# One weight load cut so that 2.5 of 8 heads come in short loads on fewer DMA engines

## Chip, cores, metric

One core of a Trainium2 chip. The metric is the device time of one execution in microseconds; the kernel before takes 206.0 us (median of 6 runs, 205.80 to 206.13). The profiled execution has a span of 204.1 us.

## The reference, cut to what matters

One decoding step of a transformer block for one token: attention of 32 heads over a cache of 4096 keys and values, the projection `wo`, a residual, then a GeGLU layer.

```python
q = (layernorm(x) @ wq)                       # 640 -> 32 heads x 128
o = softmax(q k^T * 128 ** -0.5) v            # k_cache, v_cache: 32 x 4096 x 128, bf16
h = x + o.reshape(1, 1, 32 * 128) @ wo        # wo: 4096 x 640
out = h + (gelu(ln(h) @ w_gate) * (ln(h) @ w_up)) @ w_down
```

The bytes decide it: 84.2 MB are read from HBM (the chip's large memory), 67 MB of them keys and values, and each is used once.

## The kernel before

All loads go out on one queue, that of SyncE, in the order in which they are used. `wo` comes in four groups of 8 heads, 128 partitions (rows of SBUF, the on-chip memory that the loads write) of 10240 B each. Only the group's load and the wait for it matter here.

```python
P, D, HG = 128, 640, 8
wo_t = sb("wo", [P, HG, D], bf16)

def load(name, dst, src):
    SP.dma_start(dst, src).then_inc(S[name], 16)
...
def load_wo(g):
    SP.wait_ge(S["pe"], pe_at(2 * g, "project"))
    src = A_wo[g * HG * P : (g + 1) * HG * P, :].rearrange("(p j) d -> p j d", p=P)
    load("wo", wo_t[:], src)

load("wq", wq_sb, ...)
load("x", x4[0:P:32, :], ...)                  # 4 rows
load_k(0)
for m in range(NQ):                            # 8 quads of heads
    load_k(m + 1)                              # 128 x 32768 B (cut: the last ones come in halves)
    load_v(m)
    if m % 2 == 1:
        load_wo(m // 2)
load("wg", ...); load("wu", ...)               # then w_down in six loads of 64 rows, odd and even partitions
...
if m % 2 == 1:                                 # on VectorE, before the projection
    DVE.wait_ge(S["wo"], 16)
    DVE.sem_inc(S["wo"], -16)
```

The softmax here doesn't subtract the row's maximum and nothing guards it: scores larger than these inputs give would overflow.

Of the kernel before, what the change touches and what calls it, by code (L numbers as in the profile page):

```python
# [9 lines left out]
def kernel(  # L10
# [19 lines left out]
    PE, DVE, ACT, SP, POOL = nc.tensor, nc.vector, nc.scalar, nc.sync, nc.gpsimd  # L30

    P = 128
    D = 640
# [5 lines left out]
    NQ = NH // QH  # L39
# [8 lines left out]
    PAIRS = NQ // 2  # L48
    HG = 2 * QH
    DF = 1728  # L50
    PER = 2
    PAIR_UNITS = PER * DF // P
    NFC = (PAIR_UNITS + 1) // 2
    HALVES = D // PER
    COLS = NFC * HP
    WD = ((0, 8), (8, 11), (11, 14))
    RG = DF // YR
    EPS = 1e-5
    SCALE = DH ** -0.5
    GELU_C = 0.044715  # L60
# [5 lines left out]
    def sb(name, shape, dtype=f32):  # L66
        return pool.tile(shape, dtype, name=name, tag=name)

    wo_t = sb("wo", [P, HG, D], bf16)
    TILE = NB * DH  # L70
    W_MLP = DC * DF
    big = sb("big", [P, (SLOTS + 2) * TILE + 2 * W_MLP], bf16)
# [14 lines left out]
    ones_f = sb("ones_f", [P, P])  # L87
    parity = sb("parity", [P, PER])
    mean_f = sb("mean_f", [P, P])
# [31 lines left out]
    e2 = sb("e2", [P, NFC])  # L121
    g_own = sb("g_own", [P, PER])
    hid = sb("hid", [P, NFC], bf16)
    hid_own = sb("hid_own", [P, PER], bf16)
    g_col = sb("g_col", [P, NFC, HP])
# [27 lines left out]
    S = {n: nc.alloc_semaphore(f"s_{n}") for n in names}  # L153
# [7 lines left out]
    def spare(engine):  # L161

        i = next(spares)
        return engine.memset(spare_t[:, i : i + 1], 0.0)  # L164

    def wait(engine, which, value):
        if value > 0:
            engine.wait_ge(S[which], value)
# [13 lines left out]
    def wait_pe(value):  # L182
        DVE.wait_ge(S["pe"], value)

    def dve(make, raw=True):

        if raw:
            wait(DVE, "dve", done["dve"])
        return tick("dve", make())
# [11 lines left out]
    with nc.allow_low_precision(reason="sums of one 1 and zeros"):  # L201
        dve(lambda: DVE.reduce_sum(row_of[:], by_c, AX.X), False)
        dve(lambda: DVE.reduce_sum(col_of[:], by_c.rearrange("p c j -> p j c"), AX.X), False)
        dve(lambda: DVE.reduce_sum(parity[:], ident[:].rearrange("p (i b) -> p b i", b=PER), AX.X), False)
        dve(lambda: DVE.reduce_sum(of_head[:], by_w, AX.X), False)
# [9 lines left out]
    def var_of(m, v):  # L215

        dve(lambda: DVE.tensor_tensor(v[:], m[:, 0:1], m[:, 0:1], op=ALU.mult))
        dve(lambda: DVE.tensor_tensor(v[:], m[:, 1:2], v[:], op=ALU.subtract))
        return dve(lambda: DVE.tensor_single_scalar(v[:], v[:], EPS, op=ALU.add))  # L219

# [134 lines left out]
    def pe_at(m, name):  # L355

        return T["quad", name] + m * per_turn
# [31 lines left out]
    def up(ps, w, name):  # L389
# [3 lines left out]
        for j in range(DC):  # L393
            for r in range(YR):
                rhs = w[:, j, r * RG : (r + 1) * RG].rearrange("p (i f) -> p i f", f=PAIR_UNITS)
                rhs = bass.AP(
# [54 lines left out]
    def load(name, dst, src):  # L451
        SP.dma_start(dst, src).then_inc(S[name], 16)  # L452
# [28 lines left out]

    def load_wo(g):
        SP.wait_ge(S["pe"], pe_at(2 * g, "project"))
        src = A_wo[g * HG * P : (g + 1) * HG * P, :].rearrange("(p j) d -> p j d", p=P)
        load("wo", wo_t[:], src)

    load("wq", wq_sb, A_wq.rearrange("(p c) n -> p c n", c=DC))
    SP.wait_ge(S["dve"], DVE_X4)
# [2 lines left out]
    for m in range(NQ):  # L491
        if m + 1 < NQ - 1:
            load_k(m + 1)
        else:
            load_last_k(m + 2 - NQ)
# [3 lines that stand above are left out]
# [4 lines left out]
    for i, (a, b) in enumerate(WD):  # L503
        for odd in range(PER):
            start, end_at = max(a * D, odd * HALVES), min(b * D, (NFC - 1) * D + HALVES + odd * HALVES)
            at = (PAIR_UNITS // 2) * D * odd
# [16 lines left out]
    def spread():  # L523
        shape = [P, HG, P // HG]
        return DVE.tensor_tensor(
            o_spread[:],
            o_col[:].unsqueeze(2).broadcast_to(shape),
            row_of[:].unsqueeze(1).broadcast_to(shape),
            op=ALU.mult,
        )  # L530
# [10 lines left out]
    def own_queries(m):  # L541
        shape = [P, 2, 2, QH]
        dve(
            lambda: DVE.tensor_tensor(
                q_to,
                q_at[:, m].unsqueeze(3).broadcast_to(shape),
                of_head[:].unsqueeze(1).unsqueeze(1).broadcast_to(shape),
                op=ALU.mult,
            ),
            False,  # L550
        )

    def turn_keys(m, half):
        to = kt.bitcast(f32).rearrange("p (k c j n) -> p c j k n", k=2, c=NC, n=HP)
        of = kr[m % SLOTS].bitcast(f32).rearrange("p (c x) -> p c x", c=NC)
        if half == 0 or m == NQ - 1:
            name = f"k{m % SLOTS}{'b' if half else ''}"
            DVE.wait_ge(S[name], 16)
            DVE.sem_inc(S[name], -16)
        for c in range(half * HALF, (half + 1) * HALF):  # L560
            DVE.transpose(to[:, c], of[:, c].rearrange("p (j k n) -> p j k n", k=2, n=HP)).then_inc(S["kt"], 1)  # L561
# [5 lines left out]
    for m in range(NQ):  # L567
        own = slice(QH * (m % 2), QH * (m % 2 + 1))
        wait_pe(pe_at(m, "s"))
        assert dve(lambda: DVE.transpose(s_turned[:].rearrange("p j n -> p (j n)"), s_bank[:]), False) == D_SCORES[m]  # L570
        wait_pe(pe_at(m, "e"))
        shape = [P, NB, QH]
        DVE.tensor_tensor(  # L573
            e_t[:],
            e_ps.unsqueeze(2).broadcast_to(shape),
            of_head[:].unsqueeze(1).broadcast_to(shape),
            op=ALU.mult,
        ).then_inc(S["dve_pe"], 1)
        dve(lambda: DVE.reduce_sum(rs_row[:], e_ps, AX.X), False)
        wait(DVE, "dve", done["dve"])  # L580
        DVE.tensor_scalar(rs_cur[:], of_head[:], rs_row[:], None, op0=ALU.mult).then_inc(S["dve_pe"], 1)  # L581
        if m + 1 < NQ:
            own_queries(m + 1)
            turn_keys(m + 1, 0)
        wait_pe(pe_at(m, "totals"))
        dve(lambda: DVE.reciprocal(rinv[:], t_ps), False)
        wait_pe(pe_at(m, ("pv", 1)))
        dve(lambda: DVE.tensor_tensor(o_col[:, own], o_ps, rinv[:], op=ALU.mult))  # L588
        wait(DVE, "dve", done["dve"])
        (spread() if m % 2 == 1 else spare(DVE)).then_inc(S["dve_pe"], 1)  # L590
        wait_pe(pe_at(m, "reorder"))
        if m % 2 == 1:
            DVE.wait_ge(S["wo"], 16)
            DVE.sem_inc(S["wo"], -16)
        (DVE.tensor_copy(o_row[:], r_ps) if m % 2 == 1 else DVE.memset(o_row[:], 0.0)).then_inc(S["dve_pe"], 1)  # L595
        if m + 1 < NQ:
            turn_keys(m + 1, 1)
# [81 lines left out]
```

## Time and profile before

| | before |
|---|---|
| median of 6 runs | 206.00 us |
| span of the profile | 204.1 us |
| read from HBM | 84.23 MB, 413 GB/s over the span |
| last w_down load landed | 200.68 us |
| busiest compute engine | DVE, 52% of the span |

The page's slices of the kernel before: each digit is the busy share of one fortieth of the span in tenths, for the DMA engines the mean of 16; the second line is what they moved.

```profile
DMA  7999999999998999999989999999999999999980
GB/s 249 393 475 417 411 430 469 437 411 416 437 446 381 473 450 411 424 424 456 443 370 478 437 411 430 437 443 437 395 427 424 430 433 421 433 425 429 419 369 20
```

From the second slice on, the DMA engines are busy for 80% or more of every slice but the last. The end of the chain of waits (start us, us, what) of the kernel before says the same:

```profile
175.22 0.60 SPq L452
175.82 0.04 issue
175.86 24.81 DMA big<-in_B_w_down_dram
200.68 0.04 issue
200.72 0.41 PE y L378 x12
201.13 0.02 issue
201.15 0.33 DVE y_row L630
```

The last load was issued 24.8 us before it landed: it stood in a queue. What follows it takes less than a microsecond and the store. So the kernel's time is the time at which the last of 16 DMA engines is done.

The trace also holds every DMA packet (start, duration, size, but not the engine) and every landing. Two things can be worked out from them. First, a 32768 B packet takes 1214 ns at the median (10th to 90th percentile 1213 to 1221), and most packets start 3 to 4 ns before another ends, so packets can be chained into 16 engines. Second, the 16 engines are not level. How much later than the first engine each one landed, for three loads of the kernel before (us, my tally):

```
V load, first engine at  44.3 us: 15 within 0.49, then 1.03
K load, first engine at 170.3 us: 12 within 0.46, then 0.94  1.00  1.63  2.04
w_up,   first engine at 193.4 us: 12 within 0.48, then 1.06  1.65  1.96  2.07
```

Four engines are late, and everything waits for the last. One of them started late; the other three had stood still for an instruction fetch, whose packets are on queues of their own (q8 with 16 KB, q14 with 8 KB, lines of the DMA part of the page):

```profile
q1 hardware_dynamic: 4240, 84.23, 96.7%
q8 instruction: 3, 0.05, 0.1%
q14 instruction: 2, 0.02, 0.0%
```

The columns are packets, MB and share. The share looks like nothing, but a fetch of 16 KB took about 1.09 us, one of 8 KB 0.32 us, and the load packet behind it on the same engine is stretched too (1681 ns after a 16 KB one, 1873 after the 8 KB one at 49.9 us, instead of 1213).

The load of `wo`'s first group has its issue and the next one here (SyncE's timeline of the kernel before, 53 to 60 us):

```profile
53.98 0.33 SPq L452 DMA_DIRECT2D wo<-in_A_wo_dram  x1
59.10 0.33 SPq L452 DMA_DIRECT2D big<-in_A_k_cache_dram  x1
```

### The profile page before, as it was taken

The page shows a single profiled execution, that of the slowest core. Times are in us where ns is not written, and L with a number is a line of the kernel's source. Part 1 is how long each engine was busy: PE and PEld are TensorE (multiplying, and loading weights), DVE is VectorE, ACT ScalarE, POOL GpSimd, SP SyncE. Part 2 cuts the span into 40 slices and gives each one's busy share as a digit, 9 for nine tenths or more (in the row PEclk, how much of TensorE's full clock was granted, in tenths as well). Part 3 has the DMA queues.
Part 4 walks back from the last instruction along what each step waited for, and adds up shares of the span by engine and source line. Part 5 has one row for each costly group of instructions (what it writes and reads, how often), then busy time and mean ns, then how long its engine had stood idle before and what let it go on. Part 6 is the DMA issues. An engine that isn't in the chain of part 4 may idle for free. (4 is left out here: it accounts for less than half of the span.)

```text
span 204.1 us, 4083 instructions
## 1 busy us (share of the span) xinstructions
PE 87.7 (43%) x1837; PEld 53.6 (26%) x1839; DVE 105.2 (52%) x185; ACT 4.6 (2%) x11; POOL 6.8 (3%) x12
## 2 busy tenths in 40 slices
PE   0003404406621861066407640482166468257972
PEld 0001101105311711063107310451063164046220
DVE  5003498570658278309480957065908492732360
ACT  2000100000000000000000000000000000000000
POOL 8301000000000000000000000000000000000100
PEclk9999955555585585555555555558555555555698
DMA  7999999999998999999989999999999999999980
GB/s 249 393 475 417 411 430 469 437 411 416 437 446 381 473 450 411 424 424 456 443 370 478 437 411 430 437 443 437 395 427 424 430 433 421 433 425 429 419 369 20
DMA packets 4245, 84.30 MB, mean 413 GB/s; under 512 B 528, under 2 KB 528, under 8 KB 784
## 3 DMA queue, kind: packets, MB, share of 16 engines
q1 hardware_dynamic: 4240, 84.23, 96.7%
q8 instruction: 3, 0.05, 0.1%
q14 instruction: 2, 0.02, 0.0%
HBM read 84.23 MB, written 0.00 MB: 413 GB/s over the span
## 5 line engine op out<-in xcount | busy, mean ns | idle before, releaser
L561 DVE STREAM_TRANSPOSE big<-big 128x1024 f32<-128x1024 f32 x64 | 73.8, 1211 | 6.3 <-issue 3.8
L273 PE MATMUL o<-ex,big 128*128 128x4 bf16 x1024 | 28.6, 166 | 38.7 <-PEq L173 38.7
L273 PEld LDWEIGHTS o<-ex,big 128*128 128x128 bf16 x1024 | 28.4, 104 | 39.1 <-issue 39.1
L245 PE MATMUL s<-big,q_quad 128*8 128x512 bf16 x256 | 27.9, 579 | 24.0 <-DVE big L561 24.0
L588 DVE TENSOR_TENSOR o_col<-o,rinv 128x4 bf16<-128x4 f32 x8 | 1.3, 163 | 38.9 <-PE o L273 38.9
L245 PEld LDWEIGHTS s<-big,q_quad 128*8 128x8 bf16 x256 | 7.0, 111 | 40.1 <-DVE big L561 31.9
L570 DVE STREAM_TRANSPOSE s_turned<-s 128x512 f32<-128x512 f32 x8 | 5.7, 717 | 13.5 <-PE s L245 13.5
L280 PE MATMUL a<-wo,o_row 128*1 128x160 bf16 x256 | 9.9, 333 | 2.3 <-DVE o_row L595 2.3
L573 DVE TENSOR_TENSOR ex<-e,of_head 128x512 bf16<-128x512 f32 x8 | 5.5, 692 | 6.8 <-PE e L261 6.8
L292 PE MATMUL t<-rs_cur,ones_f 128*128 128x4 f32 x16 | 4.7, 365 | 10.1 <-DVE rs_cur L581 10.1
L280 PEld LDWEIGHTS a<-wo,o_row 128*1 128x1 bf16 x256 | 7.2, 115 | 3.0 <-DVE o_row L595 3.0
L302 PE MATMUL o<-x_col,mean_f 128*128 128x10 f32 x2 | 0.6, 376 | 16.8 <-DVE x_col L210 16.8
L292 PEld LDWEIGHTS t<-rs_cur,ones_f 128*128 128x128 f32 x16 | 4.0, 312 | 11.0 <-DVE rs_cur L581 11.0
L261 PE MATMUL e<-e_part,ident 128*32 128x32 bf16 x128 | 2.5, 197 | 10.0 <-PEq L340 10.0
L445 POOL TENSOR_TENSOR hr<-hv,half_f 128x1 f32<-128x1 f32 x1 | 0.6, 554 | 172.2 <-DVE hv L219 172.2
L223 DVE CAST x_row<-x_69 128x160 f32<-128x160 bf16 x1 | 0.2, 244 | 11.6 <-DMA x_69<-in_A_x_dram 11.6
L261 PEld LDWEIGHTS e<-e_part,ident 128*32 128x32 bf16 x128 | 1.8, 106 | 16.0 <-issue 16.0
L513 ACT ACTIVATE e_part<-s_turned 128x128 bf16<-128x128 f32 x8 | 2.5, 309 | 154.1 <-DVE s_turned L570 154.1
L302 PEld LDWEIGHTS o<-x_col,mean_f 128*128 128x128 f32 x2 | 0.5, 313 | 16.8 <-DVE x_col L210 16.8
L295 PE MATMUL o<-col_of,o_spread 128*128 128x8 bf16 x8 | 1.5, 188 | 6.8 <-issue 3.3
L441 POOL MEMSET wo<- 128x5120 bf16 x1 | 4.4, 4370 | 0.0
L318 PE MATMUL g<-big,xn_bf 128*1 128x512 bf16 x20 | 2.8, 546 | 1.9 <-DVE xn_bf L230 1.9
(84 smaller groups left out, 45.7 us busy)
## 6 DMA issues: line engine op xcount, KB each, us to landing
big<-in_A_k_cache_dram SPq DMA_DIRECT2D x7, 4096.0 KB, 20.6
big<-in_A_v_cache_dram SPq DMA_DIRECT2D x6, 4096.0 KB, 17.7
big<-in_A_v_cache_dram SPq DMA_DIRECT2D x4, 2048.0 KB, 11.9
big<-in_A_wq_dram SPq DMA_DIRECT2D x1, 5120.0 KB, 15.2
wo<-in_A_wo_dram SPq DMA_DIRECT2D x4, 1280.0 KB, 15.8
big<-in_A_k_cache_dram SPq DMA_DIRECT2D x2, 2048.0 KB, 17.6
big<-in_B_w_gate_dram SPq DMA_DIRECT2D x1, 2160.0 KB, 18.5
big<-in_B_w_up_dram SPq DMA_DIRECT2D x1, 2160.0 KB, 23.2
```

The costliest lines, as they stand in the source:

```text
L245: inst = PE.matmul(s_bank[32 * r : 32 * r + 2 * QH, :], lhsT=q_quad[:, 2 * k + e, (1 - b) * QH : (3 - b) * QH], rhs=kt_at[:, k, HALF * b + ...
L261: inst = PE.matmul(to[32 * h : 32 * h + 32, r], lhsT=ident[:, 32 * r : 32 * r + 32], rhs=e_part[:, :, :, h], start=True, stop=True, tile_p ...
L273: inst = PE.matmul(o_ps, lhsT=vt[:, j, :], rhs=e_t[:, j, :], start=(j == 0), stop=(j == NB - 1))
L280: inst = PE.matmul(attn_ps[32 * r : 32 * r + 1, :], lhsT=o_row[:, j : j + 1], rhs=wo_t[:, j, r * YW : (r + 1) * YW], start=False, stop=j = ...
L292: mark("totals", PE.matmul(ps, lhsT=ones_f[:], rhs=rs_cur[:], start=True, stop=True))
L295: inst = PE.matmul(ps, lhsT=o_spread[:].rearrange("p h c -> p (h c)"), rhs=col_of[:], start=True, stop=True)
L318: inst = PE.matmul(qr_ps[b][32 * r : 32 * r + 1, :], lhsT=xn_bf[:, c : c + 1], rhs=wq_sb[:, c, :].rearrange("p (m h d) -> p m h d", h=QH, ...
L441: POOL.memset(t[:], 0.0).then_inc(S["pool"], 1)
L513: ACT.activation(e_part[:].rearrange("p b j h -> p j b h"), s_turned[:, :, 0 : 2 * QH].rearrange("p j (b h) -> p j b h", b=2), AF.Exp, sca ...
L561: DVE.transpose(to[:, c], of[:, c].rearrange("p (j k n) -> p j k n", k=2, n=HP)).then_inc(S["kt"], 1)
L570: assert dve(lambda: DVE.transpose(s_turned[:].rearrange("p j n -> p (j n)"), s_bank[:]), False) == D_SCORES[m]
L573: DVE.tensor_tensor(e_t[:], e_ps.unsqueeze(2).broadcast_to(shape), of_head[:].unsqueeze(1).broadcast_to(shape), op=ALU.mult,).then_inc(S[" ...
```

## The change

The intent, as far as the diff shows it: level the 16 engines. 40 rows can't be shared evenly by 16 engines. In the changed kernel's trace a load of 40 rows landed 10 times, one of 8 rows 8 times, one of 128 rows 16 times, so that many engines carried them. And never more than ten of the group's 3200 B packets are in flight at once there, though three loads of 40 rows stood in line: so I take it that all three ran on the same ten. The other six then have less to do. The trace gives the engines no numbers. Those here are names: 0 to 3 for the four that carry the 4 rows of x, 0 to 7 for those of the loads of 8 rows, 0 to 9 for those of 40, 10 to 15 for the rest. That each of these sets lies within the next, and is the same for every load of its size, is an assumption.

```diff
+    WO_PART = 5 * D // 2
+    WO_LOADS = [[(slice(0, P), slice(0, HG * D))] for _ in range(NQ // 2)]
+    WO_LOADS[0] = [(rows, slice(0, WO_PART)) for rows in (*[slice(i, 120, 3) for i in range(3)], slice(120, P))]
+    WO_LOADS[0] += [(slice(0, P), slice(WO_PART, HG * D))]
...
-        src = A_wo[g * HG * P : (g + 1) * HG * P, :].rearrange("(p j) d -> p j d", p=P)
-        load("wo", wo_t[:], src)
+        src = A_wo[g * HG * P : (g + 1) * HG * P, :].rearrange("(p j) d -> p (j d)", p=P)
+        dst = wo_t[:].rearrange("p j d -> p (j d)")
+        for rows, at in WO_LOADS[g]:
+            load("wo", dst[rows, at], src[rows, at])
...
-            DVE.wait_ge(S["wo"], 16)
-            DVE.sem_inc(S["wo"], -16)
+            DVE.wait_ge(S["wo"], 16 * len(WO_LOADS[m // 2]))
+            DVE.sem_inc(S["wo"], -16 * len(WO_LOADS[m // 2]))
```

## The prediction

> What bounds the kernel now: the DMA stream. In the page's slices the 16 DMA engines are about 99% busy from start to end (413 GB/s over the span), no compute engine is over 52%, and the chain of waits ends in 24.8 us of the last w_down load, landed at 200.68 us; only 0.41 us of matmul, 0.33 us of DVE and the store follow. The queue never runs dry: K and V loads land 12 to 21 us after issue.
>
> The engines run independently at one rate. In the trace's DMA packet records a 32768 B packet takes 1213 ns (10th to 90th percentile 1213 to 1221), and the last packets, when most engines have finished, are no faster. So the slowest engine sets the end, not the sum of bytes. Of each load's 16 landings 12 come within 0.48 us, four at 0.94, 1.01, 1.61 and 2.02 us. I chained packets end to start to see why: one late engine started late, the others stood still for an instruction fetch (16 KB at 50.0 and at 56.5 us, about 1.1 us each; 8 KB at 49.9 and 190.7 us). At the end these four are 1.05, 1.61, 1.92 and 2.02 us behind the first.
>
> What the change does. [...] So 128 rows use 16 engines, 40 rows 10, 8 rows 8. This trace agrees in one place: the 4-row load of x has four updates beside the sequencer's own, and four engines carry its 320 B packets. In the first 2.5 heads of group 0 (3200 B a row), engines 0-7 take 13 rows instead of 8, engines 8-9 take 12, engines 10-15 none. Bytes and matmuls stay.
>
> Cost by engine. Now: 8 packets of 10240 B at 385 ns, 3.08 us. After: 8 of 7040 B, about 267 ns (estimate between 3200 B at 126 ns and 10240 B), 2.13 us, plus 13 or 12 of 126 ns. Engines 10-15: -0.95 us; 0-7: +0.69; 8-9: +0.57. Four more issues of about 0.5 us on SP at 54 us: its next load waits until 59.1 us, so free. DVE's wait for wo lies 1.5 us after its landing: free. Only each engine's position at the end counts.
>
> So it depends on where the late four sit. The prompt twelve may take 0.69 us: they end at most 1.2 us behind the first. If all four are among 10-15, the end comes 0.95 us earlier (about 205.1 us); that is surely the intent. But the engine 1.61 us late carried a packet of x[...]. It would be 2.30 us behind, against 2.02 now: +0.3 us (206.4), even if the other three are relieved. If one of the two latest is below 10 too, +0.65 us (206.7). Chaining could have swapped two engines, and fetches could fall elsewhere, so I give the improvement 40%.
>
> Prediction: 206.2 us, 8 in 10 between 205.1 and 206.9; faster by over 2%: 1%, within 2%: 98%, slower: 1%.
>
> Signs. 192 packets of 3200 B instead of 64, 10240 B ones fewer by 128. In loads after wo group 0 the spread of landings changes: a late engine among 10-15 gains 0.95 us, one below 10 loses 0.6 to 0.7. The last w_down landing moves as the last engine's lag does.
>
> Wrong if the short loads use other engines, small packets collide on SBUF and cost over 126 ns, fetches fall on other engines, or the queue runs dry.

The sum came to 206.2 us. For an engine of 0 to 7 it is 13 packets of 126 ns less 0.95 us, +0.69 us; for the late one among them 1.61 + 0.69 - 2.02, the +0.3 us (206.4) that is weighed against a gain of 0.95 us (205.1). That loads of 40 and 8 rows use 10 and 8 engines is shown by the landings of the changed kernel (10, 10, 10 and 8).

## More of the kernel before

The columns that matter are the last two, the share of busy DMA engines and GB/s (counted by the packets that start in a stretch, so short stretches scatter by some per cent and a share may pass 1):

```profile
core 0: us, PE busy (x) PEld busy (x) DVE busy (x) ACT busy (x) POOL busy (x), PEclk, DMA share, GB/s
59.00:63.00 4.00, 0.90 (x18) 0.72 (x18) 3.11 (x7) 0.31 (x1) 0.00 (x0) 0.57 0.95 410
63.00:67.00 4.00, 1.12 (x43) 1.15 (x43) 2.76 (x4) 0.00 (x0) 0.00 (x0) 0.50 1.04 438
```

## The result

The changed kernel takes 208.26 us (median of 6 runs, 207.98 to 208.45) against 206.00 us: 2.26 us more, ratio 1.0109 (95% interval 1.0096 to 1.0122). That is within 2%, but far outside the range of the prediction. A ratio here is the mean time of one kernel's fast runs over that of the other's fast runs of the same rounds, so it is not quite the ratio of the medians.

The end of the chain of waits of the changed kernel:

```profile
177.12 0.04 issue
177.16 25.77 DMA big<-in_B_w_down_dram
202.93 0.04 issue
202.97 0.41 PE y L382 x12
203.38 0.02 issue
203.41 0.33 DVE y_row L636
```

The matmul and the addition behind the load take the same 0.41 and 0.33 us. The landing has moved from 200.68 to 202.93 us, and that is the whole difference. The loads' issue is not it. SyncE's timeline of the changed kernel, 53 to 60 us:

```profile
54.00 3.22 SPq L456 DMA_DIRECT2D wo<-in_A_wo_dram  x5
59.12 0.33 SPq L456 DMA_DIRECT2D big<-in_A_k_cache_dram  x1
```

Five issues take 3.2 us, but the next load goes out at 59.12 instead of 59.10 us, as predicted. The slices of the changed kernel:

```profile
DMA  7999999999999999999999999999999999999970
GB/s 246 437 429 406 457 451 413 406 476 430 403 413 308 467 419 413 432 464 419 413 403 460 432 445 438 413 432 445 390 436 429 419 441 422 429 425 429 423 316 10
```

The busy digits are all nines, as before. In the line below, the thirteenth slice (61.9 to 67.1 us, where the group's packets are) has 308 instead of 381 GB/s. The two stretches of the changed kernel show it better:

```profile
59.00:63.00 4.00, 0.90 (x18) 0.73 (x18) 3.11 (x7) 0.31 (x1) 0.00 (x0) 0.54 0.94 401
63.00:67.00 4.00, 0.00 (x0) 0.01 (x1) 2.77 (x4) 0.00 (x0) 0.00 (x0) 0.50 1.01 269
```

From 63 to 67 us all 16 engines are busy (share 1.01) and move 269 GB/s instead of 438. They work at packets that do not get on. In the packet records the 3200 B packets took a median 204 ns (126 at best), the 7040 B ones 335 (267 at best, 556 at worst), and four 32768 B packets of late engines, in flight at the time, took 1721 to 2062 instead of 1213 ns. Summed over 62.5 to 76.5 us against a stream of 430 GB/s, 1.54 us of the stream are lost; in the kernel before 0.00.

The landings that answer to those shown before (us behind the first engine, my tally):

```
K load, first engine at 170.9 us: 0.02 0.05, then 11 from 1.32 to 1.82, then 2.13  2.72
w_up,   first engine at 194.0 us: 0.03 0.06, then 11 from 1.31 to 1.87, then 2.20  3.75
```

Three engines run ahead: the prompt ones among the relieved. The other 13 are behind, and the last gets another microsecond between the two loads, from the 8 KB fetch at 191.8 us.

Two theories were open after this. A: engines collide where they write, so that a packet's time depends on the partitions that it and the packets beside it write. B: small pieces, or rows of HBM read in two pieces, are slow in themselves. And two sizes: how much of the 2.26 us is collisions, and how much the uneven share of a late engine among 0 to 9.

The expectations put theory A in terms of lanes: the partitions that, as I assumed, one and the same engine writes in a load of 128 rows. Which engine writes which partitions no run shows. The runs show which destinations are slow and which are not.

### The profile page after: what moved, and what is told of

Read it like the earlier page. It is cut to its first block, busy times and chain, and to the rows that moved or that the text cites. A ratio compares the mean times of both kernels' runs of the same rounds, so it can differ in the third digit from the quotient of the medians.

```text
span 206.4 us, 4089 instructions
## 1 busy us (share of the span) xinstructions
PE 89.1 (43%) x1839; PEld 53.5 (26%) x1839; DVE 105.2 (51%) x185; ACT 4.5 (2%) x11; POOL 6.8 (3%) x12
## 5 line engine op out<-in xcount | busy, mean ns | idle before, releaser
L405 PE MATMUL g<-big,hc 128*1 128x448 bf16 x20 | 3.9, 1001 | 0.1
```

Source lines behind the costliest of these rows:

```text
L405: inst = PE.matmul(ps[32 * r : 32 * r + 1, :].rearrange("q (c i b) -> q i b c", c=NFC, b=PER), lhsT=hc[:, j : j + 1], rhs=rhs, start=False ...
```

## The experiments

All kernels were correct by the comparison with the reference. For e2, e3 and e5, which leave data out on purpose, this only says that the comparison's tolerance covers the missing or misplaced part, not that the result is right. Times are medians; "lost" is lost stream time in 62.5 to 76.5 us, as above; packet times are medians.

| run | time, us | before, same rounds | ratio, 95% | 3200 B packet, ns | lost, us |
|---|---|---|---|---|---|
| changed kernel | 208.26 | 206.00 | 1.0096 to 1.0122 | 204 | 1.54 |
| e1 two pieces | 206.11 | 206.02 | 0.9988 to 1.0021 | 126 | 0.03 |
| e2 own lanes | 206.18 | 206.02 | 0.9992 to 1.0025 | 126 | 0.02 |
| e3 other lanes | 207.75 | 206.02 | 1.0071 to 1.0105 | 234 | 1.21 |
| e5 uneven, own lanes | 206.59 | 205.99 | 1.0019 to 1.0046 | 126 | 0.02 |
| e6 more on 0-3 | 206.55 | 205.99 | 1.0017 to 1.0045 | none | 0.00 |
| e7 five heads | 210.11 | 205.99 | 1.0182 to 1.0214 | 414 (6400 B) | 3.02 |
| e8 blocks of 40 | 208.38 | 205.99 | 1.0100 to 1.0131 | 155 | 1.45 |
| e9 32 rows, every fourth | 206.13 | 206.02 | 0.9997 to 1.0028 | 126 | 0.04 |
| e10 one head | 207.15 | 206.02 | 1.0045 to 1.0072 | 66 (1280 B) | 0.62 |
| e11 blocks of 32 | 208.03 | 205.94 | 1.0081 to 1.0115 | 221 | 2.10 |
| e12 every eighth | 208.06 | 205.94 | 1.0090 to 1.0134 | 205 | 2.08 |

### e1: two pieces of 128 rows

```diff
-    WO_LOADS[0] = [(rows, slice(0, WO_PART)) for rows in (*[slice(i, 120, 3) for i in range(3)], slice(120, P))]
+    WO_LOADS[0] = [(slice(0, P), slice(0, WO_PART))]
```

> Group 0 of wo as two loads of 128 rows each (3200 B and 7040 B of a row), so the pieces are cut as in the changed kernel but every engine takes 8 rows of both. Theory A (short loads make engines write partitions of other engines' SBUF lanes and they collide): no dip, 3200 B packets 126 ns, 7040 B 267 ns, time 206.1 us (before 206.0). Theory B (small pieces, or reading a row of HBM in two pieces, are slow in themselves): 3200 B packets about 200 ns and 7040 B over 400 ns as in the changed kernel, time 207.5 us or more.

206.11 us, packets of 126 and 267 ns. Small pieces cost nothing. Theory B falls.

### e2 and e3: the same loads, 64 partitions apart

```diff
+    SHIFT = 0        # e3: 64
-    WO_LOADS[0] = [(rows, slice(0, WO_PART)) for rows in (*[slice(i, 120, 3) for i in range(3)], slice(120, P))]
+    WO_LOADS[0] = [(slice(h + i, h + 32, 4), slice(0, WO_PART)) for h in (0, 32) for i in range(4)]
...
-            load("wo", dst[rows, at], src[rows, at])
+            to = slice(rows.start + SHIFT, rows.stop + SHIFT, rows.step) if rows.step else rows
+            load("wo", dst[to, at], src[rows, at])
```

> Wrong result on purpose (partitions 64 to 127 of the first 1600 columns are not loaded). Eight loads of 8 rows, each on engines 0-7[...]. Theory A: 3200 B packets stay near 126 ns and the stream stays at 425 to 432 GB/s. Theory B and a theory C (order of HBM rows): 3200 B packets slow, near 200 ns, dip of the stream to about 250 GB/s. Time by A between 205.1 and 206.2 us, as the late engines fall.

> Wrong result on purpose. Same loads, same source rows, same engines 0-7 as in e2_own_lanes; only the destination is 64 partitions higher[...]. Theory A: packets of 3200 B about 200 ns or more, 7040 B ones over 400 ns, the stream dips to about 250 to 300 GB/s, and it ends 0.8 us or more after e2_own_lanes. Theories B and C: the same as e2_own_lanes within 0.2 us, with the same packet times.

Stretches of e2:

```profile
59.00:63.00 4.00, 0.90 (x18) 0.72 (x18) 3.17 (x6) 0.28 (x1) 0.00 (x0) 0.50 0.97 418
63.00:67.00 4.00, 1.34 (x51) 1.38 (x52) 2.62 (x4) 0.00 (x0) 0.00 (x0) 0.50 1.03 430
```

Stretches of e3:

```profile
59.00:63.00 4.00, 0.90 (x18) 0.73 (x18) 3.11 (x7) 0.31 (x1) 0.00 (x0) 0.55 0.94 401
63.00:67.00 4.00, 0.14 (x5) 0.17 (x6) 2.87 (x4) 0.00 (x0) 0.00 (x0) 0.50 1.02 297
```

Same source rows, same sizes, same order, same number of engines; only the partitions written differ by 64. The stream from 63 to 67 us is 430 against 297 GB/s, a 3200 B packet 126 against 234 ns, and the time 206.18 against 207.75 us. The cause is on the side of the destination, and it depends on which partitions are written; an order of rows in HBM (theory C of the expectation) falls with it. This is the experiment that settles the kind of the loss. e2 also shows a second thing: its engines 8 to 15 have 0.95 us less to do (they miss the eight packets and have 7040 B ones for the rest), yet the end does not come earlier. So one of the latest engines is among 0 to 7.

A rival remains: that writing these partitions is slow for the engines of the short loads by themselves, without another engine in their way. The packets of e3 speak against it. The first short packet starts at 63.1 us, so no engine with eight of them can be through (8 times 126 ns) before 64.1 us. If all eight short loads run on the same eight engines, the twelve 7040 B packets that start before then must be those of the other eight, whose destination is the same as in e2, and nine of them took 400 to 529 ns instead of 267. The engines that carry none of the short loads lose too.

### e4: which engines are late

```diff
+    mark_t = sb("mark", [16, 1920], bf16)
...
         if m % 2 == 1:
             load_wo(m // 2)
+        if m == 1:
+            for k in range(1, 16):
+                load("mark", mark_t[0:k, 8 * k * (k - 1) : 8 * k * (k + 1)], A_wq[0:k, 0 : 16 * k])
```

(On the kernel before. Simplified here: the run has a semaphore of its own for these loads, and a wait for it at the end.)

> The kernel before with 15 tiny loads of 1 to 15 rows behind wo group 0 (32 B a row for each row of the load, so the size tells the load): an engine's packets tell its number. One look at which engines are the late four. My prediction's reading: one of them is among 0-3, the other three are among 10-15. Rival: the fetches fall on other engines from one execution to the next, and the changed kernel's profile already has them swapped (there the 8 KB fetches seem to hit an engine of x). Time 206 to 206.6 us.

This failed. 208.46 us in one run of unknown state: after fifteen loads of a few kB the engines were idle for part of the time (share 0.88 from 66 to 70 us, 339 GB/s). SyncE's timeline of e4:

```profile
52.83 0.33 SPq L453 DMA_DIRECT2D wo<-in_A_wo_dram  x1
53.20 5.26 SPq L453 DMA_DIRECT2D mark<-in_A_wq_dram  x15
58.51 0.40 SPq L453 DMA_DIRECT2D big<-in_A_k_cache_dram  x1
```

The K load behind them was issued at 58.5 us, yet between 66.6 and 68.5 us mostly 7 to 12 of 16 engines had a packet, and the small ones came some 0.3 us apart, load after load. The markers are too disturbed to give numbers to engines. It is a different loss from that of the change, in whose trace 16 engines are busy all the time (share 1.01 from 63 to 67 us).

The question was settled another way. In the packet records, a fetch starts 3 to 4 ns before the packet ends behind which its engine then stands still. With that rule each fetch falls on one chain. I chained all 14 profiles this way. In 12 of them, those of both kernels included, the 8 KB fetch at about 49 to 50 us stopped an engine that carries a packet of x, so one of 0 to 3; in e8 the chain broke there, and in e1 it came out as an engine without x, which I can't explain. (A second chaining, with the semaphore packets taken in and a start 2 to 5 ns before an end, gave 13 of 14, e1 and e8 included, with e4 the exception. A single chain can swap engines, so the position rests on e6 below.) The two 16 KB fetches before 60 us stopped engines without x in all 14. My first chaining, in the prediction, had swapped the two fetches that start 112 ns apart. So the engine among 0 to 3 is not the one that is 1.61 us late, but the one that the 8 KB fetches hit twice: 0.95 us late until 190.7 us, 1.92 us at the end.

### e5: the uneven share alone

```diff
 (as e2, and)
+    extra_t = sb("extra", [P, 8000], bf16)
+        if g == 0:
+            load("wo", extra_t[0:32:4, :], A_wq.rearrange("(p c) n -> p (c n)", c=DC)[0:32:4, 0:8000])
```

(The constant is written out, and VectorE's wait for the added load is left out; so in e6.)

> Wrong result on purpose. e2_own_lanes with one more load of 8 rows of 16000 B to a scratch tile[...]: these engines now take as many bytes as in the changed kernel, engines 8-15 none of it[...]. It measures the uneven share alone. If an engine among 0-3 is one of the two latest (1.92 us behind at the end in the kernel before): 206.8 us, 0.6 over e2_own_lanes. If the uneven share were the main cost of the change: 207.5 us or more. If the late engines were all among 10-15: 206.1 or less. No dip of the stream, 3200 B packets 126 ns.

206.59 us, 0.60 over the kernel before and 0.41 over e2 (0.6 were expected), without collisions (3200 B packets of 126 ns):

```profile
59.00:63.00 4.00, 0.91 (x18) 0.73 (x18) 3.11 (x7) 0.31 (x1) 0.00 (x0) 0.50 0.91 393
63.00:67.00 4.00, 1.43 (x54) 1.46 (x55) 2.85 (x4) 0.00 (x0) 0.00 (x0) 0.50 1.02 426
```

These are the stretches of e5. The uneven share costs about 0.6 us, not 2.26.

### e6: more on engines 0 to 3

```diff
 (the kernel before, and)
+    extra_t = sb("extra", [P, 9000], bf16)
+        if g == 0:
+            load("wo", extra_t[0:16:4, :], A_wq.rearrange("(p c) n -> p (c n)", c=DC)[0:16:4, 0:9000])
```

> Right result. The kernel before (wo group 0 as one load) with one load of 4 rows of 18000 B to a scratch tile[...]: engines 0-3 alone get about 0.67 us more. If one of them is 1.92 us behind at the end (the 8 KB fetches hit an engine that carries x), the end moves by 0.55 to 0.6 us: 206.6. If the one among 0-3 is 1.61 us behind, as my prediction had it: 206.3. If none of the late is among 0-3: 206.0.

206.55 us, 0.56 more. Four packets of 678 ns, on engines 0 to 3 alone, move the end by 0.56 us. So one of these four is within about 0.1 us of being the last in the kernel before, as the corrected chains say, and the prediction's 0.3 us was too small.

### e7 and e10: more and fewer bytes

```diff
-    WO_PART = 5 * D // 2
+    WO_PART = 5 * D      # e7; D in e10
```

> The changed kernel with 5 heads instead of 2.5 in the short loads (6400 B a row). Theory A (collisions in other engines' lanes, growing with the bytes): dip of the stream about twice as long (some 7 us), lost stream time about 3.1 us instead of 1.6, engines 0-3 another 0.7 us late: about 210.3 us. Rival (a fixed cost of four more loads): about 208.9 us (0.6 to 0.7 more for the uneven share only).

> The changed kernel with 1 head instead of 2.5 in the short loads (1280 B a row). If collisions and the uneven share both go with the bytes: two fifths of the 2.2 us, 206.9 us (between 206.7 and 207.1). If the loss is partly a fixed cost of the four short loads: 207.4 or more. If few bytes leave the engines apart so that they no longer collide: only the uneven share, 206.3.

With 1, 2.5 and 5 heads the kernel takes 1.13, 2.26 and 4.12 us more than before, and 0.62, 1.54 and 3.02 us of stream are lost. Loss and time go with the bytes. At one head the time lies 0.2 us over what proportion gives, and outside its range by little, so some part may be fixed; I did not look further.

### e8: blocks of 40

```diff
-    ... for rows in (*[slice(i, 120, 3) for i in range(3)], slice(120, P))]
+    ... for rows in (*[slice(i, i + 40) for i in range(0, 120, 40)], slice(120, P))]
```

> The changed kernel with three blocks of 40 adjacent partitions instead of every third. [...] If the spread by three avoids collisions: slower than the changed kernel (208.3 us) by 0.3 us or more. If engines are not in step anyway and only the share of foreign lanes counts: within 0.4 us of 208.3.

208.38 against 208.26 us. Taking every third partition buys nothing measurable.

### e9: 32 rows, every fourth partition

```diff
-    WO_LOADS[0] = [(rows, slice(0, WO_PART)) for rows in (*[slice(i, 120, 3) for i in range(3)], slice(120, P))]
+    WO_LOADS[0] = [(slice(i, P, 4), slice(0, WO_PART)) for i in range(4)]
```

> Right result. Four loads of 32 rows (every fourth partition)[...], so all 16 engines take two rows of each and the shares stay even[...]. The complement of e5_uneven_own_lanes: collisions without uneven shares. Theory A: 3200 B packets well over 126 ns, a dip of the stream that loses 1.2 us or more, all engines late together, time 207.2 to 208.2 us. If the uneven share is needed for the loss (engines 10-15 running ahead of the others): 206.1, no dip.

206.13 us and 126 ns: no collision at all, against my expectation. All 16 engines had a share of each load: the page has 64 more packets under 512 B than that of the kernel before (592 against 528), as many as the landings that four more loads on 16 engines leave (the changed kernel has 38 more, for 54 landings instead of 16). Stretches of e9:

```profile
59.00:63.00 4.00, 0.94 (x22) 0.73 (x18) 3.02 (x7) 0.31 (x1) 0.00 (x0) 0.50 0.95 410
63.00:67.00 4.00, 1.30 (x49) 1.34 (x50) 3.49 (x5) 0.00 (x0) 0.00 (x0) 0.50 1.04 433
```

Either the destination matters only for loads on fewer than 16 engines, or I had wrong which engine writes which row, and in these loads no two are in each other's way. The next two try other rows with all 16 engines: if one of them is slow, it is not the number of engines. That they would collide was an estimate from the assumed lanes.

### e11 and e12: all engines, other rows

```diff
+    WO_LOADS[0] = [(slice(i, i + 32), slice(0, WO_PART)) for i in range(0, P, 32)]     # e11
+    WO_LOADS[0] = [(slice(i, P, 8), slice(0, WO_PART)) for i in range(8)]              # e12
```

> Right result. e9_even_other_lanes showed no collision, against theory A as I had put it; but if the row order of a 16-engine load already puts every fourth partition into the engine's own lane, it was no test. Here four loads of 32 adjacent partitions: all 16 engines take two rows of each, shares even[...]. Theory A' (a lane takes what one engine gives): the stream falls to about half, 215 GB/s, 3200 B packets near 250 ns, each engine about 1.0 us late, 207.0 us. Theory D (lanes do not limit; only loads on fewer than 16 engines are slow): 126 ns, 206.1 us.

> Right result. Eight loads of 16 rows, every eighth partition, one row an engine: even shares[...]. Theory A': packets well over 126 ns, at most about 250, time 206.5 to 207.1 us (less than blocks of 32 if engines drift apart between two loads[...]). Theory D: 126 ns, 206.2 us.

Stretches of e11:

```profile
59.00:63.00 4.00, 1.15 (x22) 0.72 (x18) 2.81 (x6) 0.31 (x1) 0.00 (x0) 1.00 0.94 401
63.00:67.00 4.00, 0.00 (x0) 0.00 (x0) 3.71 (x5) 0.00 (x0) 0.00 (x0) 1.00 0.98 241
```

208.03 and 208.06 us. Every load uses 16 engines (80 and 144 landings for the group's 5 and 9 loads), and still the stream falls: with each packet's bytes spread evenly over its duration it was 217 to 222 GB/s in each half microsecond from 64 to 66 us in e11, about half of 430 (the 215 expected were an estimate from the assumed lanes). So it is which rows a load takes that counts, not the number of engines: the time is 2.1 us longer with 32 adjacent rows or every eighth one, and 0.1 us with every fourth. Why every fourth is free is not shown, as no run shows which engine writes which row. The loss of 2.1 us is twice what I expected of both: in e11 the stream stays at 218 to 319 GB/s from 65.5 to 68.5 us, when at most three engines still have short packets and the others are at 7040 B ones.

No version came out of this that beats the kernel before, and none was run as a candidate. The short loads of the changed kernel, e5 and e6 all gave more to the late engine among 0 to 3, which is 0.1 us from being the last (e6).

## Why the prediction was wrong

What held. The kernel is bound by the stream, and the last w_down landing carries the whole difference (2.25 of 2.26 us). The short loads ran on 10, 10, 10 and 8 engines: 54 landings of the group's five loads, which is 10 + 10 + 10 + 8 + 16. Packet counts came as listed (192 of 3200 B, 10240 B fewer by 128). The issues were free, and so was VectorE's wait. Three of the late engines are relieved and one is not.

The step that failed is "Engines 10-15: -0.95 us; 0-7: +0.69; 8-9: +0.57", because of its terms "13 or 12 of 126 ns" and "8 of 7040 B, about 267 ns". The 126 ns are those of a w_down load at the end of the kernel before (64 packets of 3200 B from 197.1 us on), where nothing slowed them, and the 267 ns were estimated from them. As sizes both were right where nothing collided (126 and 267 ns in e1, e2 and e5). In the change they took 204 and 335 ns at the median, and other packets in flight were stretched along. The prediction named "small packets collide on SBUF" among the things that would make it wrong, and gave it no time. It is the larger part: 1.54 us of lost stream, and nearly all of it is gone when engines 0 to 7 take as many bytes to other partitions (0.02 us in e5).

The second step is "It would be 2.30 us behind, against 2.02 now: +0.3 us". The engine among 0 to 3 is the one that was to be 1.92 us late, so the sum is 1.92 + 0.69 - 2.02 = 0.59 us. e5 measures 0.60 us for the uneven share alone, and e6 confirms the position. The caveat that chaining could have swapped two engines was right, and the check for it (fetch start against packet end) could have been made before predicting.

Together: 0.60 us (uneven share, e5) and 1.54 us (lost stream) make 2.14 of the 2.26 us. The rest is within what a mean over 16 engines can differ from the engine that ends last: between the w_up landings of the two traces that engine moved back by 2.36 us (195.36 to 197.72 us), which is 0.69 and 1.67.

Where the intended gain went: three of the four late engines were indeed relieved, and the prompt ones among 10 to 15 end 1.3 us ahead of the rest. But the end is set by the late engine among 0 to 3, which got more to do. Whether the bytes taken from one engine still get in its way at their destination was argued from the assumed lanes alone, and is not shown.

Open: why the stream stays slow for some 2 us when nearly all engines are through with the short packets (from 66.1 to 66.4 us, 13 or 14 engines with 7040 B packets of the 128-row load and two with short ones moved 226 GB/s in the changed kernel; 400 GB/s is reached at 68.0 us). No run here isolates the reason.

## What to carry to other kernels

A busy share of DMA engines did not tell their speed here (1.04 at 438 GB/s, 1.01 at 269): look at GB/s in the same stretch and at the duration of one packet of a known size. The change's loads of 40 and 8 rows slowed the whole stream here (269 instead of 438 GB/s), not only themselves; so did loads of 32 adjacent rows (241) and of every eighth row (239), while two of 128 rows (435), four of every fourth row (433) and the eight of 8 rows in e2 (430) did not. Before cutting a load, test the cut with even shares, and move its destination by 64 partitions to see whether that is at stake (430 against 297 GB/s in e2 and e3). When the last of several parallel engines sets the end, find out by a load on some of them alone (as e6) which is the last before giving anyone more to do.
